# Turning the memory attention's outputs by transposing DMAs, as f16 halves, in a two-attention Trainium2 kernel

## The chip, the cores and the metric

One core of one Trainium2 chip runs the whole program. Its engines are TensorE (PE, with its weight loads shown as PEld), VectorE (DVE), ScalarE (ACT), GpSimd (POOL) and SyncE (SP), which here issues every DMA of the program. The metric is the device time of one execution in microseconds (us). The kernel before takes 1773.4 us, the median of three executions that lie between 1772.57 and 1774.67 us.

## The reference, cut to what matters

Two independent attentions over 2048 positions, 1024 features and 32 heads of 32; their outputs stand side by side. The change concerns A, which walks four segments of 512 positions with a compressive memory:

```python
for s in range(4):
    qs, ks, vs = q[:, :, s], k[:, :, s], v[:, :, s]
    p = softmax(qs @ ks.T * scale + mask)          # causal inside the segment
    a_dot = p @ vs
    pq = phi(qs)                                    # t+1 if t>0 else exp(t)
    a_mem = (pq @ M) / (pq @ z + 1e-6)              # M, z from the earlier segments
    outs.append(g * a_mem + (1 - g) * a_dot)
    M = M + phi(ks).T @ vs;  z = z + phi(ks).sum(0)
a = concat(outs) @ wo
```

B projects q, k and v, maps q and k through a per-head weight and two softmaxes (of +t and -t), forms linear attention with the sums over all positions, and projects with its own `wo`.

## The kernel before, in words

**Arithmetic.** Matrices are kept as two f16 tiles, a high half and the rest, and each product is made of three f16 matmuls (`product`, L352). To fit f16, a tensor is first scaled by a bound on its size (`halves`, L376: ScalarE writes the scaled high half, VectorE the scaled rest). B's projections and A's output projection use seven block products in place of eight (`strassen`, L541, and the last loop of the file).

**Stages.** First come A's 32 units, each one segment s (512 positions) of one group g of four heads (L582). Unit u is made by `produce` (L710: k, q and v projections, halves, three stacked copies of q and of k sent by DMAs at L727) and `attend` (L740). While unit u attends, the engines also produce unit u+1, fold B's feature weights (`fold`, L969) and load later weights. Then, for eight pairs of B's 128-row tiles, the k and v projections, softmaxes and sums (L1214 on); then, for 16 tiles, the q side and B's output projection (L1385 on). Here the normalised features are split into halves and turned by `dma_start_transpose` (L1440) before a matmul reads them. Last comes A's output projection: eight steps c of the loop at L1463, each with a row tile c and a row tile c+8.

**The place of the change.** At the end of `attend`, VectorE forms the local part in `osum` (L926), for s > 0 GpSimd adds the memory part `amem` (L930), and the sum, positions in partitions, must be turned so that features are in partitions. TensorE does this with four f32 transposes into a PSUM bank (L935), ScalarE copies the bank to `oT` (L603, through `copy`), and SP stores `oT` as f32 in the DRAM scratch `oa_d` (L937). The output stage loads two row tiles of `oa_d` (L1467), VectorE makes four sums and differences (L1473), and `halves` scales and splits seven operands by the reciprocal of one bound of the whole tensor, `osc2[:, 0]` (lines L386 and L388 in the profile); then come 7 x 12 matmuls at L1502. That bound is the running maximum `big` of the value bounds, filled in `bounds_v` (L673).

**What sets the order.** Nothing runs in the order in which it is written. Every `op(...)` gives an engine, an estimated duration, the buffers that it reads and writes, a priority `prio` (a lower number first), for DMAs a latency `lat` and a size `kb`. `Graph.run` (L148) simulates the engines with these numbers at build time: it takes the engine that can start earliest, and among what could start then the lowest `prio`. The result is a fixed order on each engine and on SP's queue; on the chip each engine follows its order and waits where something is late. A DMA's data is planned for its issue duration, plus a term for the bytes at 230 GB/s, plus `lat`. An `op` with `port=True` on VectorE and all on GpSimd are planned not to overlap. A tag with `bufs=1` has one buffer: the next user of the tag waits for all uses of the one before. The priority of unit u is 2u in `produce` and 2u+1 = P in `attend`.

```python
    def buf(self, pool, shape, dtype, tag, bufs=1):
        q = self.tags.setdefault(tag, [])
        b = Buf(lambda: self.pools[pool].tile(shape, dtype, name=tag, tag=tag, bufs=bufs),
                (q[-bufs] if len(q) >= bufs else None, q[-1] if q else None, self.opened.get(pool)))
...
                flow = max(flow, free[e]) + o.kb / self.FLOW
                o.lat += flow - free[e]
```

A's stage keeps its tiles in a pool "a" and B's in a pool "b" that takes the same memory; `G.control(swap, ["b"])` lets tiles of "b" be planned only once every operation listed before it has been started in the plan.

Of the kernel before, what the change touches and what calls it, by code (L numbers as in the profile page):

```python
# [8 lines left out]
F32 = mybir.dt.float32  # L9
# [234 lines left out]
def tile_kernel(ctx: ExitStack, tc: tile.TileContext, ax, aw, awv, awo, beta, bx, bwqk, bwv, bphi, bwo, out):  # L244
# [7 lines left out]
    oa_d = dram.tile([NT, 128, NG, 128], F32, name="oa_d")  # L252
# [46 lines left out]
    osc2 = const.tile([128, 2, 2], F32, name="osc2")  # L299
    nc.gpsimd.memset(causal[:, 0:384], 0.0)  # L300
# [295 lines left out]
    bigs, swfs, wscs, oscs, phss = (G.fixed(t) for t in (big, swf, wsc, osc2, phs))  # L596
# [76 lines left out]
    def bounds_v(k, segs, prio):  # L673
# [5 lines left out]
        for x in segs:  # L679
# [8 lines left out]
            big[:, 0:1], bv()[:, 1, a:a + 1], bv()[:, 1, b:b + 1], big[:, 0:1], op0=OP.max, op1=OP.max), r=w, w=[(bigs, 0)], prio=prio)  # L688
        op(POOL, 0.4, lambda: nc.gpsimd.tensor_scalar(bv()[:, 0, v], xsc[:, s0:s0 + n, 0], wvs[:, kk, 0:1], None, op0=OP.mult),
           r=[*((xscs, x) for x in segs), (wvss, kk)], w=w, prio=prio)  # L690

    def values(u):
# [7 lines left out]
        op(POOL, 0.39, lambda: nc.gpsimd.tensor_scalar(sc(), gate1[:, 4 * g:4 * g + 4], bv()[:, 1, i2:i2 + 1], None, op0=OP.mult),  # L700
           r=[gates, (bv, i2)], w=[sc], prio=P + VPRIO)
# [38 lines left out]
    def attend(u):  # L740
        s, g = units[u]
        d, P = un.pop(u), 2 * u + 1
        st, vl, vf, bd, bv, i2 = stk[u % 3], vlb[u % 2], vfb[u % 3], bds[group(u)], d["bv"], s % 2
        KR, QR = [(st, (1, r)) for r in range(3)], [(st, (0, r)) for r in range(3)]
# [71 lines left out]
        if s > 0:  # L816
            amem = G.buf("a", [128, 4, 4, 32], F32, "amem", 1)
            for b in range(2):
                ps = bank("misc", [128, 2, 132], "memory")
                for i in range(2):  # L820
# [5 lines left out]
                dve(0.1, lambda ps=ps, dm=dm: nc.vector.tensor_scalar(dm(), ps()[:, :, 128:132], 1e-6, None,  # L826
                                                                       op0=OP.add), r=[ps], w=[dm])
# [104 lines left out]
        oT = G.buf("a", [128, 4, 128], F32, "oT", 1)  # L932
        po = bank("misc", [128, 4, 128], "output")
        for i in range(4):
            pe(0.112, lambda i=i: nc.tensor.transpose(po()[:, i, :], osum()[:, i, :], ident), r=[osum], w=[po], need=[oT])  # L935
        act(0.48, copy(oT, po), r=[po], w=[oT])
        op(SP, 0.6, lambda: nc.sync.dma_start(oa_d[4 * s:4 * s + 4, :, g, :].rearrange("c p t -> p c t"), oT()),  # L937
           r=[oT], w=[(osc, u)], prio=P, lat=1.5)
# [446 lines left out]
    for c in range(NT):  # L1385
# [25 lines left out]
        for hb in range(2):  # L1411
# [27 lines left out]
            for a in range(2):  # L1439
                op(SP, 0.6, lambda a=a, eh=eh, hb=hb, pt=pt: nc.sync.dma_start_transpose(pt()[:, a], eh()[:, hb, a]),  # L1440
                   r=[(eh, (hb, a))], w=[(pt, a)], prio=P, lat=2.0, kb=256)
# [132 lines left out]
```

## Time and profile before

| | |
|---|---|
| median of three executions | 1773.4 us (1772.57 to 1774.67) |
| profiled execution, its own time | 1776.28 us |
| its span on the core | 1774.3 us |
| busy: PE, DVE, ACT, POOL | 1692.8, 1472.0, 1129.0, 942.9 us |
| mean granted TensorE clock | 0.987 |

The profiled execution took 2.9 us more than the median. "Busy" counts a matmul from its start to its modelled end, and consecutive matmuls overlap, so a PE that is busy all the time can still be short of its full rate. `L935` in a row is line 935 of the kernel; `misc<-ident,osum` names the tile written and the tiles read; `x128` is a count; after the bar of a group come busy time and the mean duration of one in ns, and after the next bar the engine's idle time just before them with what ended it. In a row of the stages, the numbers behind each engine are its busy time and, in brackets, its instructions. In a chain, the work that ended last is followed back through what released it.

### The profile page before, as it was taken

To read this page: it belongs to the slowest core of one execution; us is meant where nothing else is said; L and a number is where in the kernel's file an instruction comes from. 1 tells how busy PE (TensorE), PEld (TensorE's weight loads), DVE (VectorE), ACT (ScalarE), POOL (GpSimd) and SP (SyncE) were. 2 spreads that over 40 slices of the span, in tenths; PEclk is the share of its full clock that TensorE was granted. 3 is DMA by queue.
4 is the path that set the end of the run, shared out by engine and by line. 5 is a ranking of instruction groups with operands and counts; after the bars stand their busy time and mean duration, and the time that the engine had idled before them with its cause. 6 is when DMAs were issued, how large, how long until landed. Compare 5 with 4: busy or idle time off the path is not lost.

```text
span 1774.3 us, 38460 instructions
## 1 busy us (share of the span) xinstructions
PE 1692.8 (95%) x14456; PEld 1013.7 (57%) x14456; DVE 1472.0 (83%) x3335; ACT 1129.0 (64%) x2063; POOL 942.9 (53%) x1141
## 2 busy tenths in 40 slices
PE   7999998999999999999989998999889899999999
PEld 5767766677776766676644444444544344444444
DVE  6989989899787888788877999997999889887541
ACT  6897886988766878688673755554644454444431
POOL 6445454555757677867583544443467778640000
PEclk9999999999999999999989999999999999999999
DMA  6546545574545453665465344266455555565311
GB/s 204 175 144 182 161 144 161 167 222 141 148 139 150 112 158 107 173 210 144 153 192 203 113 160 161 90 234 243 153 139 132 158 146 148 137 190 172 119 66 65
DMA packets 240842, 275.67 MB, mean 155 GB/s; under 512 B 137488, under 2 KB 190480, under 8 KB 231952
## 3 DMA queue, kind: packets, MB, share of 16 engines
q1 hardware_dynamic: 240656, 273.22, 49.9%
q8 instruction: 113, 1.85, 0.4%
q14 instruction: 73, 0.60, 0.1%
HBM read 145.44 MB, written 85.00 MB: 130 GB/s over the span
## 4 chain that ended last, share of the span: by engine, by line
PE 46%; DVE 31%; ACT 5%; issue 3%; POOL 2%; DMA 2%; SPq 0%; DVEq 0%; ACTq 0%; POOLq 0%
PE proj L359 17%; PE proj L549 5%; PE proj L1502 5%; DVE r L1122 4%; DVE mx L1112 3%; DVE e L1116 3%; PE pv L903 3%; PE s L867 3%; PE s L1502 2%; DVE s L775 2%; DVE S L388 2%; PE s L769 2%; DVE e L1114 2%; DVE dn L1419 2%; DVE kls L1437 2%
## 5 line engine op out<-in xcount | busy, mean ns | idle before, releaser
L359 PE MATMUL proj<-S,S 128*128 128x128 f16 (+1 forms) x3072 | 503.1, 299 | 5.6 <-ACT S L386 3.6
L359 PEld LDWEIGHTS <-S 128*128 128x128 f16 x4608 | 331.4, 99 | 154.1 <-issue 9.7
L549 PE MATMUL proj<-S,S 128*128 128x512 f16 x1488 | 352.5, 385 | 24.3 <-ACT cs L555 12.1
L549 PEld LDWEIGHTS <-S 128*128 128x128 f16 x1968 | 189.5, 99 | 247.3 <-issue 35.2
L880 POOL TENSOR_SCALAR_AFFINE_SELECT ph<-ph 128x256 f16<-128x256 f16 (+1 forms) x448 | 197.1, 462 | 174.4 <-DVE ph L874 137.4
L874 DVE SCALAR_TENSOR_TENSOR ph<-s,ph 128x512 f16<-128x512 f32 x320 | 210.4, 683 | 58.3 <-ACT ph L873 56.4
L775 DVE CUSTOM_DVE_ANT_0 s<-s,causal 128x512 f32<-128x512 f32 (+3 forms) x512 | 242.2, 510 | 12.5 <-PE s L769 9.1
L871 ACT ACTIVATE s<-s,bd 128x512 f32<-128x512 f32 x320 | 212.2, 708 | 23.0 <-PE s L867 22.6
L873 ACT ACTIVATE ph<-s 128x512 f16<-128x512 f32 x320 | 189.9, 652 | 0.9 <-PE pv L903 0.3
L1119 ACT ACTIVATE e<-e,sk 128x256 f32<-128x256 f32 x256 | 114.6, 500 | 99.6 <-DVE e L1116 96.5
L359 PE MATMUL misc<-S,ot 128*128 128x512 f16 x768 | 172.4, 382 | 1.9 <-DVE ot L1454 1.4
L359 PEld LDWEIGHTS <-ot 128*128 128x128 f16 x768 | 74.0, 98 | 92.3 <-DVE ot L1454 2.4
L769 PE MATMUL s<-S 96*128 96x512 f16 (+3 forms) x512 | 113.3, 300 | 5.8 <-DVE mt L775 4.2
L867 PE MATMUL s<-S 104*128 104x512 f16 (+3 forms) x512 | 114.5, 302 | 1.2 <-DVE quad L1011 0.5
L1416 POOL TENSOR_TENSOR e<-e,zb 128x512 f32<-128x512 f32 x64 | 90.9, 1441 | 46.3 <-DVE r L1122 40.7
L359 PE MATMUL proj<-wv,S 128*128 128x128 f16 x1536 | 104.2, 221 | 0.3 <-DVE mt L775 0.3
L903 PEld LDWEIGHTS <-ph 128*128 128x128 f16 x2560 | 87.6, 96 | 17.9 <-issue 1.9
L1226 POOL TENSOR_TENSOR e<-e,r 128x1024 f32<-128x1024 f32 x32 | 64.5, 2020 | 61.2 <-DVE r L1125 50.4
L903 PE MATMUL pv<-vl,ph 128*128 128x66 f16 (+1 forms) x2560 | 92.7, 185 | 2.1 <-POOL ph L880 1.3
L1429 POOL TENSOR_TENSOR e<-e,r 128x1024 f32<-128x1024 f32 x32 | 67.4, 2113 | 37.7 <-DVE r L1427 34.4
L1122 DVE TENSOR_REDUCE r<-e 128x32 f32<-128x1024 f32 x64 | 76.8, 1204 | 9.8 <-ACT e L1119 9.8
L549 PE MATMUL s<-S,S 128*128 128x512 f16 x324 | 77.1, 379 | 1.8 <-ACT cs L555 1.8
(300 smaller groups left out, 3294.0 us busy)
## 6 DMA issues: line engine op xcount, KB each, us to landing
S<-h SPq DMA_DIRECT2D x192, 128.0 KB
S<-wf_d SPq DMA_DIRECT2D x21, 1024.0 KB
st<-bwqk SPq DMA_DIRECT2D x64, 256.0 KB
wf_d<-fo SPq DMA_DIRECT2D x48, 256.0 KB
out<-os SPq DMA_DIRECT2D x40, 256.0 KB
wf_d<-oT SPq DMA_DIRECT2D x36, 256.0 KB
S<-xf_d SPq DMA_DIRECT2D x9, 1024.0 KB
S<-aw SPq DMA_DIRECT2D x16, 512.0 KB
```

Of the source, the lines that this page charges most:

```text
L359: op(PE, dur, lambda c=c, a=a, b=b, lv=lv, rv=rv: nc.tensor.matmul(pv(), lv(), rv(), start=(c == 0 and a + b == 0), stop=(c == n - 1 and a ...
L549: op(PE, 0.215, lambda n=n, a=a, b=b, lv=lv, rv=rv: nc.tensor.matmul(ps(), lv(), rv(), start=(start and n == 0 and a + b == 0), stop=(n == ...
L769: nc.tensor.matmul(ps()[:, o:o + 128 * i + 128], st()[0:96, 0, h, 128 * i:128 * i + 128], st()[0:96, 1, h, 0:128 * i + 128], start=True, s ...
L775: dve(0.12 + 0.00113 * n, lambda h=h, i=i, o=o, n=n: nc.vector.tensor_tensor_reduce(ps()[:, o:o + n], ps()[:, o:o + n], causal[:, 512 - n: ...
L867: nc.tensor.matmul(ps()[:, o:o + n], st()[0:104, 1, h, 128 * j:128 * j + 128], st()[0:104, 0, h, 128 * j:512], start=True, stop=True)
L871: act(0.59, lambda: nc.scalar.activation(ps(), ps(), AF.Exp, bias=0.0, scale=bd()[:, 4, i2, 0:1]), r=[(bd, i2)], w=[ps])
L873: act(0.5, lambda: nc.scalar.activation(ph()[:, 0], ps(), AF.Copy, scale=2.0 ** 14), r=[ps], w=[(ph, 0)])
L874: dve(0.6, lambda: nc.vector.scalar_tensor_tensor(ph()[:, 1], ps(), 2.0 ** 14, ph()[:, 0], op0=OP.mult, op1=OP.subtract), r=[ps, (ph, 0)], ...
L880: nc.gpsimd.affine_select(pd, pd, pattern=[[0, n], [1, 128]], compare_op=OP.is_ge, fill=0.0, base=0, channel_multiplier=-1)
L903: nc.tensor.matmul(ps()[:, i, n0:n1], ph()[:, a, o:o + 128], vl()[:, j, h, n0:n1], start=(i == 0 and a == 0), stop=(j == min(i, 2)), skip_ ...
L1122: op(DVE, 1.13, lambda: nc.vector.tensor_reduce(r(), e(), axis=AX.X, op=OP.add), r=[e], w=[r], prio=prio)
L1502: op(PE, 0.215, lambda n=n, a=a, b=b: nc.tensor.matmul(ps(), v(a)[:, n, :], wform[w]()[:, b, n, :], start=(start and n == 0 and a + b == 0 ...
```

## The change

Per unit, the four TensorE transposes, their PSUM bank and ScalarE's copy out of it go. Instead ScalarE copies `osum` to an f16 high half, GpSimd subtracts to give the f16 rest, both in a tile `oh` on the tag "pkt" (the tag of the turned keys, one buffer), and SP issues one transposing DMA for each half into `oT`, now f16, and then the store to `oa_d`, which holds two f16 halves in the room of one f32. These operations have priority P + 3.2 in place of P.

The outputs are kept divided by a running maximum: `bounds_v` keeps in `top` the largest value bound up to each segment and in `part` the ratio of the segment's own bound to it; `sc` (the factor of the local part) uses `part`, and the memory part's denominator is multiplied by `top`. After B's q side, `top` is multiplied once by the reciprocal of the whole tensor's bound.

In the output stage each row tile is loaded as two quarter-size f16 pairs on the tag "cs"; VectorE adds each pair to f32, and ScalarE multiplies by `top` (two instructions for each pair). The sums and differences follow as before; the seven operands are then split without a scale (a ScalarE copy, a VectorE subtraction). All of this preparation has priority P - 1.5 in place of P. Lastly the planned duration of the existing transposing DMAs at L1440 is set from 0.6 to 1.25.

```diff
-    oa_d = dram.tile([NT, 128, NG, 128], F32, name="oa_d")
+    oa_d = dram.tile([NT, 2, 128, 4, 2, 128], F16, name="oa_d")
...
+        for x in segs:
+            op(DVE, 0.07, lambda x=x: nc.vector.tensor_tensor(
+                top[:, kk, x + 1:x + 2], top[:, kk, x:x + 1], bv()[:, 1, x % 2:x % 2 + 1], op=OP.max), r=w, w=[(tops, kk)], prio=prio)
+        op(DVE, 0.1, lambda: nc.vector.reciprocal(part[:, kk, s0:s0 + n], top[:, kk, s0 + 1:s0 + n + 1]), r=[(tops, kk)], w=[(parts, (kk, s0))], prio=prio)
+        op(DVE, 0.07, lambda: nc.vector.tensor_tensor(part[:, kk, s0:s0 + n], part[:, kk, s0:s0 + n], bv()[:, 1, v], op=OP.mult),
+           r=w, w=[(parts, (kk, s0))], prio=prio)
...
-        op(POOL, 0.39, lambda: nc.gpsimd.tensor_scalar(sc(), gate1[:, 4 * g:4 * g + 4], bv()[:, 1, i2:i2 + 1], None, op0=OP.mult),
-           r=[gates, (bv, i2)], w=[sc], prio=P + VPRIO)
+        op(POOL, 0.39, lambda: nc.gpsimd.tensor_scalar(sc(), gate1[:, 4 * g:4 * g + 4], part[:, k % 4, s:s + 1], None, op0=OP.mult),
+           r=[gates, *[(parts, (k % 4, y)) for y in ((0, 1) if s < 2 else (2,)) if y <= s]], w=[sc], prio=P + VPRIO)
...
-                dve(0.1, lambda ps=ps, dm=dm: nc.vector.tensor_scalar(dm(), ps()[:, :, 128:132], 1e-6, None,
-                                                                       op0=OP.add), r=[ps], w=[dm])
+                dve(0.1, lambda ps=ps, dm=dm: nc.vector.tensor_scalar(
+                    dm(), ps()[:, :, 128:132], 1e-6, top[:, kk, s + 1:s + 2], op0=OP.add, op1=OP.mult), r=[ps, (tops, kk)], w=[dm])
...
-        oT = G.buf("a", [128, 4, 128], F32, "oT", 1)
-        po = bank("misc", [128, 4, 128], "output")
-        for i in range(4):
-            pe(0.112, lambda i=i: nc.tensor.transpose(po()[:, i, :], osum()[:, i, :], ident), r=[osum], w=[po], need=[oT])
-        act(0.48, copy(oT, po), r=[po], w=[oT])
-        op(SP, 0.6, lambda: nc.sync.dma_start(oa_d[4 * s:4 * s + 4, :, g, :].rearrange("c p t -> p c t"), oT()),
-           r=[oT], w=[(osc, u)], prio=P, lat=1.5)
+        oh = G.buf("a", [128, 2, 512], F16, "pkt", 1)
+        oT = G.buf("a", [128, 4, 2, 128], F16, "oT", 1)
+        op(ACT, 0.52, lambda: nc.scalar.activation(oh()[:, 0], osum().rearrange("p c n -> p (c n)"), AF.Copy), r=[osum], w=[(oh, 0)], prio=P + 3.2)
+        op(POOL, 1.25, prio=P + 3.2, fn=lambda: nc.gpsimd.tensor_tensor(oh()[:, 1], osum().rearrange("p c n -> p (c n)"), oh()[:, 0], op=OP.subtract),
+             r=[osum, (oh, 0)], w=[(oh, 1)])
+        for a in range(2):
+            op(SP, 1.25, lambda a=a: nc.sync.dma_start_transpose(oT()[:, :, a, :], oh()[:, a]), r=[(oh, a)], w=[(oT, a)],
+               prio=P + 3.2, lat=2.0, kb=128)
+        op(SP, 0.6, lambda: nc.sync.dma_start(
+            oa_d[4 * s:4 * s + 4, g // 4, :, g % 4].rearrange("c p a t -> p c (a t)"), oT().rearrange("p c a t -> p c (a t)")),
+           r=[oT], w=[(osc, u)], prio=P + 3.2, lat=1.5)
...
+    op(DVE, 0.1, lambda: nc.vector.tensor_scalar(top, top, osc2[:, 0, 1:2], None, op0=OP.mult), r=[(oscs, 0)], w=[tops], prio=P)
...
-                op(SP, 0.6, lambda a=a, eh=eh, hb=hb, pt=pt: nc.sync.dma_start_transpose(pt()[:, a], eh()[:, hb, a]),
+                op(SP, 1.25, lambda a=a, eh=eh, hb=hb, pt=pt: nc.sync.dma_start_transpose(pt()[:, a], eh()[:, hb, a]),
...
-            op(SP, 0.6, lambda t=t, k=k: nc.sync.dma_start(t().rearrange("p h g t -> p (h g) t"), oa_d[k]),
-               r=[osc], w=[t], prio=P, lat=1.0, kb=512)
+            for h in range(2):
+                hl = G.buf("b", [128, 4, 2, 128], F16, "cs", 4)
+                op(SP, 0.6, lambda hl=hl, k=k, h=h: nc.sync.dma_start(
+                    hl().rearrange("p g a t -> p (g a t)"), oa_d[k, h].rearrange("p g a t -> p (g a t)")),
+                   r=[osc], w=[hl], prio=P - 1.5, lat=1.0, kb=256)
+                op(DVE, 0.6, lambda t=t, h=h, hl=hl: nc.vector.tensor_tensor(t()[:, h], hl()[:, :, 0], hl()[:, :, 1], op=OP.add),
+                   r=[hl], w=[(t, h)], prio=P - 1.5)
+                for i in range(2):
+                    op(ACT, 0.4, lambda t=t, h=h, i=i, k=k: nc.scalar.activation(
+                        t()[:, h, 2 * i:2 * i + 2], t()[:, h, 2 * i:2 * i + 2], AF.Copy, scale=top[:, 2 * h + i, k // 4 + 1:k // 4 + 2]),
+                       r=[*((tops, y) for y in range(4))], w=[(t, h)], prio=P - 1.5)
...
-               r=[A0, A1, *[(ss, i) for i in range(k)]], w=[(ss, k)], prio=P)
+               r=[A0, A1, *[(ss, i) for i in range(k)]], w=[(ss, k)], prio=P - 1.5)
...
-            halves(*hl, ((src, k) if src is ss else src, half(src, k)), (oscs, 0, lambda: osc2[:, 0]), 512, P)
+            op(ACT, 0.52, lambda hl=hl, src=src, k=k: nc.scalar.activation(hl[0][2](), half(src, k)(), AF.Copy),
+               r=[(src, k)], w=[hl[0][:2]], prio=P - 1.5)
+            op(DVE, 0.6, lambda hl=hl, src=src, k=k: nc.vector.tensor_tensor(hl[1][2](), half(src, k)(), hl[0][2](), op=OP.subtract),
+               r=[(src, k), hl[0][:2]], w=[hl[1][:2]], prio=P - 1.5, port=True)
```

6 lines of the change are left out of this document (5 added, 1 removed).

## The prediction

> **What bounds the kernel now.** I read the busy times by stage first: A's units with a full pipeline, A's end, B's k side, B's q side, the join of that with A's output projection, and the projection.
>
> ```profile
> 60.00:860.00 800.00, 787.62 (x8550) 561.07 (x8548) 685.01 (x1956) 630.82 (x1147) 488.63 (x758) 1.00 0.53 155
> 860.00:945.00 85.00, 76.91 (x658) 43.97 (x656) 67.39 (x162) 59.85 (x105) 55.97 (x81) 0.94 0.61 202
> 945.00:1300.00 355.00, 329.07 (x2167) 163.78 (x2166) 322.88 (x556) 196.30 (x406) 157.04 (x114) 0.99 0.46 166
> 1300.00:1600.00 300.00, 278.19 (x1845) 131.05 (x1844) 275.25 (x412) 139.13 (x250) 205.14 (x133) 0.99 0.55 149
> 1600.00:1625.00 25.00, 24.89 (x166) 11.69 (x166) 19.76 (x29) 12.50 (x19) 0.52 (x1) 0.93 0.68 211
> 1625.00:1774.00 149.00, 145.26 (x674) 65.68 (x671) 59.98 (x88) 50.30 (x77) 0.00 (x0) 1.00 0.23 85
> ```
>
> Behind each stretch and its length stand PE, PEld, DVE, ACT and POOL, then the granted clock, the DMA share and GB/s. From 60 to 860 PE idles 12.4 us in 800; DVE has 115 us left, ACT 169, POOL 311. From 945 to 1600 PE and DVE are both at 91 to 93%. From 1625 PE is full but for the last copy and store. So PE work taken out before 860 can shorten the program, work added to ACT, DVE or POOL there should find room, and the output stage gets shorter only if its matmuls do.
>
> Then PE's waits between 60 and 860, to see whether an engine that is about to get more work already holds PE up, and the part of the chain that ended last behind 1600.
>
> ```profile
> PE s L769 <- DVE mt L775: 4.2, 9, 0.9
> ...
> PE misc L837 <- POOL sc L700: 0.5, 1, 0.5
> ...
> PE misc L795 <- DVE mh L790: 0.2, 1, 0.2
> ```
>
> ```profile
> by line: PE proj L1502 47.6%; PE s L1502 23.8%; PE misc L359 13.1%; PE misc L1502 11.9%; DMA pt<-kls 2.9%; PE pv L1448 1.4%; ACT os L1509 0.4%; issue 0.1%; ACTq L1509 0.0%
> ```
>
> The columns of the waits are us in all, times and the longest. The table has 18 rows, from the first to the last shown; the row with POOL is the only one with it, all the others name DVE, and none names a DMA. The chain behind 1600 has no preparation of the output stage in it, only matmuls, one DMA of the q side and the last copy.
>
> **The change, part by part.**
>
> (1) The transposes. Four instances in a row, and what follows them on PE:
>
> ```profile
> 559.85 0.60 PE L935 MATMUL misc<-ident,osum 128*128 128x128 f32 x4
> 560.28 0.50 PE L822 MATMUL misc<-mem,pq 128*128 128x132 f32 x3
> ...
> 60.00:860.00 800.00, 17.56 (x116) 13.44 (x116) 1.00 0.53 155
> 860.00:945.00 85.00, 1.81 (x12) 1.42 (x12) 0.94 0.61 202
> ```
>
> The next matmul starts 0.43 us after the first transpose: that is what a unit's four transposes take from PE. Their busy time alone, in the last two rows, is 17.56 us for 116, 0.61 a unit, but its ends overlap the next matmul's start, so 0.43 is the price and 0.61 the upper end. 116/4 = 29 units lie before 860: 29 x 0.43 = 12.5 us (17.6 at most; 0 if something else paces the units). The three units behind 860 lie where PE has 8 us of idle; I count nothing for them.
>
> (2) Copies and subtractions in the units. Rows of the same forms:
>
> ```profile
> L603 ACT ACTIVATE oT<-misc x32: 577/597/777, 88.8 to 942.2; 128x512 f32<-128x512 f32 x32
> L1256 ACT ACTIVATE pt<-e x64: 613/622/632, 966.6 to 1272.4; 128x512 f16<-128x512 f32 x64
> L1259 POOL TENSOR_TENSOR pt<-e,pt x32: 1152/1162/2712, 968.8 to 1269.0; 128x512 f16<-128x512 f32 x32
> L683 DVE TENSOR_SCALAR bv<-misc x9: 150/152/160, 28.4 to 714.3; 128x2 f32<-128x2 f32 x7, 128x1 f32<-128x1 f32 x2
> L826 DVE TENSOR_SCALAR dm<-misc x48: 111/160/167, 91.3 to 915.7; 128x8 f32<-128x8 f32 x48
> ```
>
> ACT exchanges 0.597 for 0.622, 0.8 us in 32 units. POOL gains 32 x 1.162 = 37 us, against 311 idle. What stands behind a subtraction on POOL is mostly the causal masks (L880) that PE's `pv` waits for; if each subtraction delayed PE by its whole length it would cost 37 us, but POOL is 61% busy and none of PE's waits above is on a mask, so I take 0. `bounds_v` runs 9 times (the count of L683) and gains 16 maxima, 9 reciprocals and 9 products, 34 x 0.152 = 5.2 us of DVE, hidden in its 115 (5.2 if not). `dm` gets a second operation in an instruction of 0.16 us that stays one instruction: 0.
>
> (3) The DMAs. The trace has transposing DMAs of twice the size in the q side, and shows how long after its issue the matmul behind one starts:
>
> ```profile
> L1440 SPq DMA_TRANSPOSE pt<-kls x64: 1231/1248/5174, 1290.8 to 1607.6; - x64
> ...
> 1427.06 1.23 SPq L1440 DMA_TRANSPOSE pt<-kls  x1
> ...
> 1431.06 0.86 PE L1448 MATMUL pv<-pt,st 128*64 128x128 f16 x24
> ...
> 1595.09 1.23 SPq L1440 DMA_TRANSPOSE pt<-kls  x1
> ...
> 1600.11 0.61 PE L1448 MATMUL pv<-pt,st 128*64 128x128 f16 x15 [3.52 <-DMA pt<-kls]
> ```
>
> 64 new ones take 64 x 1.25 = 80 us of SP (40 if half the bytes halve the issue; I take 80, the row's own value), and the data is there 4.0 us after the start of the issue, or 5.0 behind a load: 2.8 to 3.8 us behind its end. Three things wait: the store behind them on SP, with every DMA behind it, above all the stacked copies of q and k (L727); the next unit's turned keys, on the tag "pkt"; and the fold's halves on the tag "oT". SP waits already, in the same stretch of the program:
>
> ```profile
> SPq L962 <- POOL oT L466: 56.8, 15, 10.9
> SPq L962 <- POOL ph L880: 52.8, 19, 8.5
> SPq L937 <- ACT oT L603: 48.9, 21, 9.1
> SPq L727 <- ACT h L721: 40.7, 16, 11.0
> ```
>
> These come to 199 us, with PE hardly waiting, so the plan keeps distance between SP and PE, and the store's own wait on ScalarE (48.9) goes for one on a DMA. A unit takes 800/29 = 27.6 us, and the keys need their tag once in it. I take 1 us for new stalls (0 to 40: one issue of 1.25 us on PE's path in each of 32 units; a gain is excluded, since SP gets only more).
>
> The Trainium skill speaks against this part: VectorE: DVE Perf Modes, section The three transpose paths, gives 390 ns for a 128x128 transpose on TensorE and 1309 ns by DMA, and its rules for kernel authors take TensorE where PSUM will do. The trace has 270 ns for one on TensorE, pitch 0.11, and 1.25 us of issue for eight blocks by DMA. An estimate by that page, eight half-blocks of a unit each 1309 ns on the path, is 10.5 us a unit, 335 us in all; Advanced Engine Details and Errata, section X-Bar Transpose, has them as fast as ordinary DMAs instead. What decides is not the transfer but who waits for it.
>
> (4) The hand-over to B. Tiles of "b" are planned only once the last store is.
>
> ```profile
> 939.39 1.27 POOL L930 TENSOR_TENSOR osum<-osum,amem 128x512 f32<-128x512 f32 x1 [2.49 <-DVE osum L926]
> ...
> 942.17 2.75 PE L549 MATMUL misc<-S,S 128*128 128x512 f16 x12
> 942.65 0.59 ACT L555 ACTIVATE cs<-proj 128x512 f32<-128x512 f32 x1
> 944.70 0.39 SPq L937 DMA_DIRECT2D oa_d<-oT  x1
> 944.76 2.75 PE L549 MATMUL s<-S,S 128*128 128x512 f16 x12
> 947.35 1.03 PE L549 MATMUL proj<-S,S 128*128 128x512 f16 x4
> ```
>
> `osum` is done at 940.66; then 0.62 (copy), 1.16 (subtraction), 1.25 (issue) and 2.8 (landing) put the store at 946.5, against 944.70, and the first copy into "b", now 942.65, up to 4 us later. PE has two products of 2.59 us (942.17, 944.76) that need no tile of "b" as cover; I take +2 (0 to 4).
>
> (5) The output stage.
>
> ```profile
> L1119 ACT ACTIVATE e<-e,sk x256: 492/498/516, 957.2 to 1582.5; 128x256 f32<-128x256 f32 x128
> L1473 DVE TENSOR_TENSOR zb<-e x8: 679/684/1923, 1599.1 to 1676.5; 128x512 f32<-128x512 f32 x8
> L386 ACT ACTIVATE ot<-e,osc x16: 706/712/723, 1582.9 to 1721.7; 128x512 f16<-128x512 f32 x16
> L388 DVE SCALAR_TENSOR_TENSOR ot<-e,osc,ot x16: 744/748/754, 1587.7 to 1722.5; 128x512 f16<-128x512 f32 x16
> ```
>
> A step gains 4 x 0.684 on DVE and loses 7 x (0.748 - 0.684): +2.3 us, 18 in eight steps, on a stretch where DVE is busy 60.0 of 149. ACT gains 8 x 0.498 and loses 7 x (0.712 - 0.622): +3.4, 27 in all, on 50.3. PE keeps its 84 matmuls a step, 145.26 us for eight, so the stage stays at PE's length. If that cover were gone the cost would be 27. The first step is prepared while the q side, at 92% of DVE, ends: its four additions (2.7) and eight copies (4.0) can stand ahead of the last tile's output copies. I take +1 (0 to 4).
>
> (6) The planned 1.25 at L1440 removes and adds nothing; it lets the plan order the q side otherwise. The nearest rows are the DVE's 24.8 us of idle in those 300 and the wait of 3.5 at 1600.11: -10 to +10, since no reason excludes either sign; I take 0.
>
> Sum: -12.5 + 1 + 2 + 1 = -8.5. The profiled execution of 1776.28 (span 1774.3 and 2.0 around it) would become 1767.8; it lies 2.9 over the median, so the median goes from 1773.4 to 1764.9, say 1765.
>
> **The rivals.**
>
> *The transposes paid on SP's queue (slower).* SP issues in order, and a store that waits 2.8 us or more for its transposes holds the stacked copies of the next q and k. The point from which it decides is 0.43 us of PE wait a unit. With one issue of 1.25 in each unit's path: -12.5 + 32 x 1.25 + 3 = +30, 1804; with half of it 1784. For it: up to 10.9 us of one wait on this queue, and the 5174 ns of one issue. Against it: the PE waits above, none on a DMA. The page that prefers TensorE would give this side. Chance 0.14.
>
> *PE does not pace the units (no change).* Busy time counts overlapping ends, and if the units hang on the exchange between scores and DVE, the 12.5 us turn into idle time: 1773.4 + 1 (in the terms above, +4 at most). For it: DVE's 86%, and the wait on `mt` as the longest. Against it: 12.4 us of idle in 800. Chance 0.15, at 1774.
>
> *The reordered B stages lose.* Stages of PE and DVE at 92% may lose by another order: 1765 + 10 + 2 = 1777. Chance 0.07; the same reorder as a gain, 1765 - 10 = 1755, has 0.12.
>
> **How the numbers follow.** My forecast itself has 0.52, with its own range of 1759 to 1769.8: from 0.61 a unit with nothing lost to two thirds of the gain. 0.2% of the time before, 3.5 us, is about what a measurement of this kernel can tell from no change. Faster: 0.52 + 0.12 = 0.64. Same: 0.15, less a little that falls over the line, and near misses of the forecast: 0.15. Slower: 0.14 + 0.07 = 0.21. The range from 1753 to 1784 holds the forecast, the gain, the unchanged case, the reorder and the smaller price of the queue; the full price, some 0.1, and a tail below stay out.
>
> **What would show it.** Right: no matmul at L935 and PE as full as before in the units, which reach B's k side some 10 us earlier; then equal lengths of B's stages, and a projection of 145 us on PE without gaps. Wrong: waits of PE on a DMA or on the keys' bank, longer waits of L727 on SP, `pv` waiting for masks behind a subtraction, a gap of PE where "b" opens, or a first output step that waits for its additions and copies.

## The result and the profile after

The changed kernel takes 1779.65 us (median of six executions, 1774.76 to 1781.28), the kernel before beside it 1774.51 (six, 1772.57 to 1775.26). The ratio is 1.0028 with a 95% interval of 1.0015 to 1.0041: slower by 0.3%, where 1765 was forecast. The time lies inside the stated range of 1753 to 1784, on the side that had a chance of 0.21. The profiled execution of the changed kernel took 1779.33 us, its span is 1777.4 (before 1774.3), its mean granted clock 0.983 (before 0.987).

The busy times by stage of the changed kernel, in the columns used before:

```profile
60.00:860.00 800.00, 779.15 (x8399) 545.58 (x8396) 696.37 (x1994) 631.05 (x1140) 508.01 (x781) 0.98 0.60 163
860.00:945.00 85.00, 77.88 (x674) 45.36 (x672) 69.43 (x170) 61.70 (x108) 65.08 (x89) 0.98 0.72 208
945.00:1300.00 355.00, 329.77 (x2156) 163.66 (x2155) 323.06 (x546) 195.41 (x406) 156.32 (x118) 0.98 0.49 170
1300.00:1600.00 300.00, 282.57 (x1874) 132.83 (x1873) 277.67 (x431) 146.69 (x263) 201.42 (x134) 1.00 0.61 156
1600.00:1625.00 25.00, 22.18 (x152) 10.26 (x152) 23.51 (x34) 16.26 (x33) 4.62 (x2) 0.93 0.52 133
1625.00:1777.00 152.00, 148.40 (x688) 67.07 (x686) 71.94 (x111) 63.34 (x119) 0.00 (x0) 1.00 0.26 90
```

The transposes are gone, yet the units are not shorter. From 60 to 945 PE executed 8399 + 674 = 9073 matmuls, before 9208; the difference of 135 is the 128 transposes and seven more, so by the records both kernels stand at about the same place at 945. PE idles 885 - 857.0 = 28.0 us in this stretch against 20.5 before, and the trace has it at half clock for 30.7 us there against 17.1. If PE does half as much in a stretch at half clock, the 13.6 us more cost 6.8, an estimate. So 7.5 of idle time and these 6.8, 14.3 together, stand against the 32 x 0.43 = 13.8 us of transposes. The saving is spent where it was made.

The rest moved little. VectorE's last local part starts at 943.0 (938.6 before), the first copy into "b" at 947.5 (942.65), the last matmul of the q side ends at 1616.4 (1612.2), and from there to the end are 161.0 us (162.1).

PE's waits from 60 to 945 now have 26 rows in place of 23; the first four, and the one on the keys' tile:

```profile
PE pv L914 <- POOL ph L891: 3.3, 5, 1.1
PE misc L806 <- DVE mh L801: 3.0, 4, 1.4
PE pv L914 <- DVE ph L885: 2.9, 6, 1.2
PE s L780 <- DVE mt L786: 2.8, 4, 1.8
...
PE misc L853 <- ACT pkt L606: 0.4, 1, 0.4
```

Masks on GpSimd (L891) now lead; before they made 1.3 us in three waits. Waits on a DMA, none before, come to 1.7 us in two, and the one on the keys' tile to 0.4, so little says that a DMA or the keys hold PE up. That is misleading, as the experiments show: PE's order is written at build time, so work that the plan had to put later isn't waited for on the chip; PE does other work first and runs out of it later. What shows it is progress, for instance how many of the 24 turned keys (the copies into `pkt`) were made by 430.5 us. First the kernel before, then the changed one, in the rows by tile:

```profile
L603 ACT ACTIVATE pkt<-misc x15: 578/643/842, 46.8 to 430.4; 128x512 f32<-128x512 f32 x15
```

```profile
L606 ACT ACTIVATE pkt<-misc x12: 575/598/777, 48.7 to 423.3; 128x512 f32<-128x512 f32 x12
```

Three keys fewer. The 430.5 is set just behind the fifteenth key of the kernel before; the changed kernel makes its fifteenth at 476.8. The first and second half of the units show what that does to PE, before and after:

```profile
60.00:430.00 370.00, 360.19 (x3879) 258.26 (x3877) 335.97 (x925) 305.29 (x555) 186.52 (x313) 0.99 0.55 166
430.00:860.00 430.00, 427.42 (x4672) 302.81 (x4671) 349.04 (x1032) 325.53 (x593) 302.11 (x445) 1.00 0.51 146
```

```profile
60.00:430.00 370.00, 350.75 (x3633) 241.19 (x3630) 334.57 (x944) 299.46 (x540) 185.25 (x320) 0.96 0.61 169
430.00:860.00 430.00, 428.40 (x4768) 304.39 (x4766) 361.79 (x1051) 331.60 (x600) 322.76 (x462) 1.00 0.59 157
```

From 430 on PE is full in both kernels. Before 430 its idle time grows from 9.8 to 19.3 us and its clock falls from 0.99 to 0.96.

The reason can be followed in the timelines (start, duration, engine, line, operation). First the second unit's keys and the first unit's outputs, before and after:

```profile
66.88 0.60 ACT L603 ACTIVATE pkt<-misc 128x512 f32<-128x512 f32 x1
...
88.78 0.60 ACT L603 ACTIVATE oT<-misc 128x512 f32<-128x512 f32 x1 [2.87 <-PE misc L935]
```

```profile
93.32 0.63 ACT L945 ACTIVATE pkt<-osum 128x512 f16<-128x512 f32 x1 [2.33 <-DVE osum L937]
...
103.96 0.60 ACT L606 ACTIVATE pkt<-misc 128x512 f32<-128x512 f32 x1
```

The buffer of a tag goes round in the order in which the program lists its users, and the first unit's halves are listed ahead of the second unit's keys. Before, keys ran ahead of the outputs of the unit before; now they stand behind them. In the changed kernel every copy of a unit's keys starts behind the halves of the unit before, and so it does in all its draws below.

Then a stretch of the changed kernel on ScalarE's `pkt` tiles and SP's queue:

```profile
254.71 0.72 ACT L606 ACTIVATE pkt<-misc 128x512 f32<-128x512 f32 x1
261.69 0.63 ACT L945 ACTIVATE pkt<-osum 128x512 f16<-128x512 f32 x1 [1.04 <-DVE osum L937]
...
268.99 0.55 SPq L977 DMA_DIRECT2D wf_d<-oT  x1
...
277.61 0.55 SPq L977 DMA_DIRECT2D wf_d<-oT  x1
...
285.22 2.54 SPq L949 DMA_TRANSPOSE oT<-pkt  x2
...
293.20 0.57 ACT L606 ACTIVATE pkt<-misc 128x512 f32<-128x512 f32 x1
```

The outputs take the one buffer of "pkt" at 261.69, right behind the keys of 254.71. Before they can be turned they need the one buffer of "oT", which fold's halves use for two more stores; the transposes go out at 285.22, and the next keys are copied at 293.20. Keys are 38.5 us apart here, where the pace of a unit is 27.6; these, the eighth, come at 293.20, and before at 229.1. In 11 of the 32 units the halves lie in "pkt" for over 10 us before the second transpose is issued, at most 35.5. The outputs hold "oT" longer too: from ScalarE's copy to the issue of the store the median unit takes 0.6 us before, and from the first transposing issue to that of the store 6.4 after.

The hand-over to B:

```profile
943.02 0.68 DVE L937 TENSOR_TENSOR osum<-oall,rd 128x512 f32<-128x512 f32 x1
943.78 1.27 POOL L941 TENSOR_TENSOR osum<-osum,amem 128x512 f32<-128x512 f32 x1 [2.49 <-DVE osum L937]
945.08 0.63 ACT L945 ACTIVATE pkt<-osum 128x512 f16<-128x512 f32 x1 [0.66 <-POOL osum L941]
945.79 1.16 POOL L946 TENSOR_TENSOR pkt<-osum,pkt 128x512 f16<-128x512 f32 x1 [0.74 <-ACT pkt L945]
946.72 2.93 SPq L949 DMA_TRANSPOSE oT<-pkt  x2
947.46 0.57 ACT L558 ACTIVATE cs<-proj 128x512 f32<-128x512 f32 x1
...
954.55 0.37 SPq L951 DMA_DIRECT2D oa_d<-oT  x1
```

The store goes out 9.9 us later than before (944.70), but the first copy into "b" follows the last local part by 4.4 us, 0.4 more than before (942.65 - 938.6): the new store doesn't hold it up.

The output stage: the added preparation by line (count, min/median/max ns, first and last start), and PE's waits at the join, 1590 to 1640.

```profile
L1488 DVE TENSOR_TENSOR e<-cs x32: 678/684/1229, 1581.7 to 1690.6; 128x512 f32<-128x512 f16 x32
L1491 ACT ACTIVATE e<-e,top x64: 492/496/510, 1583.0 to 1692.3; 128x256 f32<-128x256 f32 x64
```

```profile
PE pv L1464 <- DMA pt<-kls: 3.5, 2, 2.6
PE misc L362 <- DVE ot L1470: 1.2, 1, 1.2
PE proj L1530 <- ACT ot L1521: 0.9, 1, 0.9
PE proj L1530 <- DVE ot L1523: 0.3, 1, 0.3
PE misc L362 <- ACT ot L1468: 0.2, 1, 0.2
```

The durations are those of the forecast. At the join, 2.6 us of waits on late halves are new beside the 3.5 that were there (before, one wait of 3.5 on the same DMA); behind it PE is full.

### The profile page after: what moved, and what is told of

Same layout as the page of the kernel before. It is cut to its first block, busy times and chain, and to the rows that moved or that the text cites. A ratio compares the mean times of both kernels' runs of the same rounds, so it can differ in the third digit from the quotient of the medians.

```text
span 1777.4 us, 38464 instructions
## 1 busy us (share of the span) xinstructions
PE 1691.2 (95%) x14328; PEld 1001.3 (56%) x14328; DVE 1502.1 (85%) x3403; ACT 1153.1 (65%) x2127; POOL 970.2 (55%) x1173
## 5 line engine op out<-in xcount | busy, mean ns | idle before, releaser
L552 PE MATMUL proj<-S,S 128*128 128x512 f16 x1488 | 347.2, 382 | 12.6 <-ACT cs L558 7.9
L891 POOL TENSOR_SCALAR_AFFINE_SELECT ph<-ph 128x256 f16<-128x256 f16 (+1 forms) x448 | 192.0, 449 | 163.2 <-DVE ph L885 145.7
L786 DVE CUSTOM_DVE_ANT_0 s<-s,causal 128x512 f32<-128x512 f32 (+3 forms) x512 | 243.5, 507 | 20.3 <-PE s L780 16.8
L884 ACT ACTIVATE ph<-s 128x512 f16<-128x512 f32 x320 | 186.2, 637 | 0.7 <-PE pv L914 0.2
L552 PE MATMUL s<-S,S 128*128 128x512 f16 x324 | 78.9, 385 | 3.8 <-ACT cs L558 3.8
```

The source lines that it names most:

```text
L552: op(PE, 0.215, lambda n=n, a=a, b=b, lv=lv, rv=rv: nc.tensor.matmul(ps(), lv(), rv(), start=(start and n == 0 and a + b == 0), stop=(n == ...
L786: dve(0.12 + 0.00113 * n, lambda h=h, i=i, o=o, n=n: nc.vector.tensor_tensor_reduce(ps()[:, o:o + n], ps()[:, o:o + n], causal[:, 512 - n: ...
L884: act(0.5, lambda: nc.scalar.activation(ph()[:, 0], ps(), AF.Copy, scale=2.0 ** 14), r=[ps], w=[(ph, 0)])
L891: nc.gpsimd.affine_select(pd, pd, pattern=[[0, n], [1, 128]], compare_op=OP.is_ge, fill=0.0, base=0, channel_multiplier=-1)
```

## The experiments

All medians stand beside the kernel before on the same chip (1774.2 to 1775.8); ratios carry a 95% interval. Two questions are asked: what each part costs with the order of the instructions kept, and what the order does.

**The transposes alone, in the order before.** The four matmuls keep their places in the plan but aren't executed, and ScalarE copies `osum` itself.

```diff
-            pe(0.112, lambda i=i: nc.tensor.transpose(po()[:, i, :], osum()[:, i, :], ident), r=[osum], w=[po], need=[oT])
-        act(0.48, copy(oT, po), r=[po], w=[oT])
+            pe(0.112, lambda: None, r=[osum], w=[po], need=[oT])
+        act(0.48, copy(oT, osum), r=[po], w=[oT])
```

> The kernel before, in its own order, with the four transposes of each unit not executed: ScalarE copies osum itself, so A's outputs are stored unturned and A's result is meaningless; all else is kept. If PE paces the units (the prediction's part 1), 12.5 us go: 1762, at most 17.6. If chains of the other engines pace them in a fixed order, under 4 us go: 1771 to 1774.

1767.26 us, 0.9954 (0.9939 to 0.997): 7.5 us off by the medians, between the two cases expected. Then the same with the order planned anew, without the transposes and their bank:

```diff
-        po = bank("misc", [128, 4, 128], "output")
-        for i in range(4):
-            pe(0.112, lambda i=i: nc.tensor.transpose(po()[:, i, :], osum()[:, i, :], ident), r=[osum], w=[po], need=[oT])
-        act(0.48, copy(oT, po), r=[po], w=[oT])
+        act(0.48, copy(oT, osum), r=[osum], w=[oT])
```

> The same work left out (outputs unturned, A's result meaningless), but the order is planned anew without the transposes and their bank. If PE paces the units and a new order costs nothing, the same 1762 as with the old order. If a new order moves the time by itself, the two differ by 5 us or more, either way.

1764.63 us, 0.994 (0.9923 to 0.9957): 10.1 us off, 2.6 from the run with the old order. PE does pace the units, at least in part, and its transposes are worth 7.5 to 10 us by the medians, less than the 12.5 of the sum; the second interval reaches 13.7, and it is one order of many. So the change loses some 12 to 15 us elsewhere.

**The added work, in the order after.** GpSimd's subtraction becomes a memset of the low half:

```diff
-        op(POOL, 1.25, prio=P + 3.2, fn=lambda: nc.gpsimd.tensor_tensor(oh()[:, 1], osum().rearrange("p c n -> p (c n)"), oh()[:, 0], op=OP.subtract),
+        op(POOL, 1.25, prio=P + 3.2, fn=lambda: nc.gpsimd.memset(oh()[:, 1], 0.0),
```

> The changed kernel in its own order; GpSimd writes zeros for the low half in place of the subtraction, so the low halves of the memory attention's outputs are left out. If GpSimd's 32 subtractions of 1.16 us hold up DVE's small instructions and the masks, 5 to 10 us come back: 1770 to 1775. If the time is lost in the order and in the shared buffers, under 3 us: 1777 to 1780.

1774.94 us, 1.0003 (0.9993 to 1.0012), against 1.0028 for the change: 0.25%, some 4.4 us, come back when the instruction shrinks from 1.158 to 0.524 us. That lies between the two cases expected.

Plain DMAs in place of the transposing ones:

```diff
-            op(SP, 1.25, lambda a=a: nc.sync.dma_start_transpose(oT()[:, :, a, :], oh()[:, a]), r=[(oh, a)], w=[(oT, a)],
+            op(SP, 1.25, lambda a=a: nc.sync.dma_start(oT()[:, :, a, :], oh()[:, a].rearrange("p (c n) -> p c n", c=4)), r=[(oh, a)], w=[(oT, a)],
```

> The changed kernel in its own order; each transposing DMA is a plain DMA of the same bytes, so A's outputs are stored unturned and A's result is meaningless. If the transposing DMAs' 1.25 us of issue and their landing hold the SP queue on PE's path, 5 to 15 us come back: 1765 to 1775. If SP's waits are only idle time of the queue, under 3 us: 1777 to 1780.

1777.09 us, 1.0013 (1.0002 to 1.0023). The issues of the two kernels, the changed one first:

```profile
L949 SPq DMA_TRANSPOSE oT<-pkt x64: 1188/1244/2500, 94.0 to 948.4; - x64
```

```profile
L949 SPq DMA_DIRECT2D oT<-pkt x64: 599/629/1337, 94.2 to 948.8; - x64
```

SP's 64 issues take half the time, and 0.15% (2.7 us) comes back, with intervals that overlap: the case of under 3. So the length of the issues isn't where the time is. The order on the queue, and how long a DMA at its head waits for its data, are the same in both runs and aren't tested by this.

Both replacements together:

> The changed kernel in its own order with both left out: zeros for the low halves and plain DMAs in place of transposing ones (A's outputs stored unturned and without their low halves). If the two costs in the same order add up, 4.7 + 2.5 = 7 us come back: 1772 to 1773, and what is left to the 1767 of the kernel before without its transposes is the order's. If they are one and the same idle time, 5 us: 1775.

1776.24 us, 1.0012 (1.0002 to 1.0021): 0.16% back, 2.8 us, less than the memset alone gave and below both cases expected; the interval overlaps that of the change. The effects don't add up, and none of them reaches the missing 12.

The output stage without ScalarE's 64 scalings by `top`, whose places in the plan stay:

```diff
-                    op(ACT, 0.4, lambda t=t, h=h, i=i, k=k: nc.scalar.activation(
-                        t()[:, h, 2 * i:2 * i + 2], t()[:, h, 2 * i:2 * i + 2], AF.Copy, scale=top[:, 2 * h + i, k // 4 + 1:k // 4 + 2]),
+                    op(ACT, 0.4, lambda: None,
```

> The changed kernel in its own order without ScalarE's 64 scaling copies in the output stage, so A's outputs stay unscaled and A's result is wrong. If these copies hold up the last tiles of the q side (the step priced +1, at most 4), 2 to 4 us come back: 1775.5 to 1777.5. If they hide, under 1 us: 1779 to 1780.

1777.98 us, 1.0017 (1.0003 to 1.0031): 0.11% back, not told apart from none and between the two cases expected. What is missing isn't in the length of these instructions; the order is tried next.

**Other orders of both kernels.** Every planned duration is multiplied by a random factor between 0.99 and 1.01. The instructions stay the same; the plan comes out in another order.

```diff
+import random
+NOISE = random.Random(1)
...
-        o.eng, o.dur, o.fn, o.prio, o.lat, o.kb = eng, dur, fn, (prio, len(self.ops)), lat, kb
+        o.eng, o.dur, o.fn, o.prio, o.lat, o.kb = eng, dur * (1 + 0.01 * NOISE.uniform(-1, 1)), fn, (prio, len(self.ops)), lat, kb
```

> The kernel before, the same instructions; each planned duration is multiplied by a random factor between 0.99 and 1.01 (first draw), so that the builder arrives at another order. If a new order by itself moves the time by as much as the change did, this lies 3 us or more from 1774.5, either way. If the order hardly matters, within 2 us.

> As the first draw of the kernel before, with a second draw: 1770 to 1780 if orders scatter by some 5 us; within 2 us of 1774.5 if they hardly matter.

> The kernel before, third draw: 1769 to 1781 as its other orders.

The kernel before, seeds 1 to 3: 1780.67 us, 1.0029 (1.0017 to 1.0041); 1770.83, 0.9972 (0.9955 to 0.9989); 1762.73, 0.9932 (0.9913 to 0.9952). The third lies 6 us under the range expected for it.

> The changed kernel, the same instructions, its planned durations multiplied by the same kind of random factors (first draw). If the change as such costs what was measured, about 5 us over the kernel before with its draw. If the change binds orders by its shared single buffers and its own order is a fortunate one, 10 to 25 us over the kernel before's draws: 1785 to 1800. If the order is all, it lies among the kernel before's draws.

> As the first draw of the changed kernel, with a second draw: 1785 to 1800 if the shared buffers bind the orders; 1775 to 1785 if the change costs what was measured with any order.

> The changed kernel, third draw of random factors. If its own order is a fortunate one among those that its buffers allow, 1790 to 1810 as the other two draws. If the first two draws were bad luck, 1775 to 1785.

The changed kernel: 1810.31 us, 1.0191 (1.0155 to 1.0227); 1799.66, 1.0131 (1.0102 to 1.0161); 1806.51, 1.0179 (1.0159 to 1.0199). The first lies 10 us over the 1785 to 1800 expected.

Identical instructions spread over 18 us by their order, more than all that was forecast of the change. But the two kernels' draws don't overlap: 1771.4 on average before, 1805.5 after. By these averages of three the change costs some 34 us, and the changed kernel as it stands, 26 us below its draws, has a fortunate order. The own order of before lies inside its draws.

**Own buffers.** First only the halves leave the keys' tag, for a tag "os" whose buffer lies in another pool:

```diff
-        oh = G.buf("a", [128, 2, 512], F16, "pkt", 1)
+        oh = G.buf("stage", [128, 2, 512], F16, "os", 1)
```

> The changed kernel with the halves alone on a buffer of their own (the idle output tile of the stage pool), the turned halves still on the fold's tag; first draw. If sharing the keys' buffer is what binds, about as low as with both buffers (1761 to 1787); if sharing the fold's binds, 1800 to 1810 as the changed kernel's draws; if each does half, 1780 to 1795.

> The changed kernel with the halves alone on a buffer of their own, second draw. If each of the two shared buffers does about half, the three draws average 1785 to 1795; if the keys' buffer does nearly all, under 1782; if the fold's, over 1798.

> The same, third draw: the three draws average 1785 to 1795 if each shared buffer does about half, under 1782 if the keys' buffer does nearly all, over 1798 if the fold's.

1786.25 us, 1.0065 (1.0045 to 1.0085); 1799.32, 1.014 (1.0111 to 1.017); 1800.86, 1.0149 (1.012 to 1.0179): 1795.5 on average, half a microsecond over the range for "half each". Draw by draw that is 24.1, 0.3 and 5.7 us below the changed kernel, so on the time alone this step isn't told apart from the scatter of orders. Then `oT` has a tag of its own too; to make room, `ph` goes from six buffers to five:

```diff
-            ph = G.buf("a", [128, 2, 512], F16, "ph", 6)
+            ph = G.buf("a", [128, 2, 512], F16, "ph", 5)
...
-        oh = G.buf("a", [128, 2, 512], F16, "pkt", 1)
-        oT = G.buf("a", [128, 4, 2, 128], F16, "oT", 1)
+        oh = G.buf("stage", [128, 2, 512], F16, "os", 1)
+        oT = G.buf("a", [128, 4, 2, 128], F16, "oT2", 1)
```

> The changed kernel with buffers of their own for the new tiles (the halves on the idle output tile of the stage pool, the turned halves on a new tag; to make room the probability halves have five buffers in place of six), first draw of random factors. If the shared single buffers bind the orders, it lies 15 us or more under the changed kernel's draw (1810): below 1795, and three such draws lie around the kernel before's. If the new operations themselves cost the time, within 8 us of the changed kernel's draws.

> The same kernel with its own buffers, second draw: 15 us or more under the changed kernel's draws (1800 to 1810) if the shared buffers bind the orders, within 8 us of them if not.

> The same kernel with its own buffers, third draw: 15 us or more under the changed kernel's draws (1800 to 1810) if the shared buffers bind the orders, within 8 us of them if not.

1760.69 us, 0.9926 (0.9903 to 0.9949); 1787.26, 1.0071 (1.0043 to 1.0099); 1779.87, 1.0032 (1.002 to 1.0045): 1776.0 on average, 30 below the shared tags; draw by draw 49.6, 12.4 and 26.6, of which the second misses the 15 asked for. Even so the average lies 4.5 us above that of the kernel before and not below it. The first of them beats both kernels as they stand; the best order of before, at 0.9932, can't be told from it.

The traces of these orders say what the tags did. Each column gives the kernel's own order, where it was run, and the draws 1, 2, 3:

| | before | after | halves on "os" | both on own tags |
|---|---|---|---|---|
| time, us | 1774.5; 1780.7, 1770.8, 1762.7 | 1779.7; 1810.3, 1799.7, 1806.5 | 1786.3, 1799.3, 1800.9 | 1760.7, 1787.3, 1779.9 |
| keys made by 430.5 us | 15; 15, 15, 15 | 12; 12, 13, 12 | 15, 15, 15 | 15, 15, 15 |
| PE busy of 370, 60 to 430 | 360.2; 363.1, 365.4, 366.5 | 350.8; 352.3, 352.8, 348.5 | 360.8, 362.3, 355.8 | 365.9, 364.4, 362.5 |
| last keys copied, at us | 849; 842, 843, 837 | 895; 896, 903, 913 | 841, 838, 857 | 845, 824, 846 |
| last fold copy into "oT" | 904; 897, 898, 884 | 913; 912, 921, 931 | 908, 903, 921 | 846, 831, 866 |
| first copy into "b" | 942.7; 946.0, 938.4, 933.7 | 947.5; 955.9, 962.5, 971.4 | 952.0, 945.1, 963.6 | 917.9, 925.3, 941.1 |
| from there to the end | 831.7; 830.2, 831.4, 829.7 | 829.9; 850.0, 836.2, 833.7 | 835.0, 852.6, 836.6 | 839.9, 859.8, 835.7 |

The keys' tag: with the halves elsewhere the keys are back on their old times in all three draws (the second at 66 to 68 us, the fifteenth at 415 to 430, in place of 94 to 105 and 473 to 478), and PE gets most of its busy time before 430 back. The fold's tag: with `oT` elsewhere fold ends some 63 us earlier, and the gap that late folds leave in front of "b" narrows: PE is busy for 64.5, 67.7 and 69.2 of the 85 us from 860 with the halves on "os", for 78.9, 73.5 and 75.2 with both. The rows from 860 to 945 of draw 1, halves on "os" first, then both:

```profile
860.00:945.00 85.00, 64.50 (x479) 33.65 (x477) 50.96 (x121) 53.41 (x97) 56.04 (x78) 0.78 0.62 184
```

```profile
860.00:945.00 85.00, 78.91 (x533) 39.95 (x531) 63.75 (x135) 50.96 (x93) 46.84 (x61) 0.96 0.75 221
```

On average of three draws "b" opens at 939.4 before, 963.3 after, 953.6 with the halves on "os", 928.1 with both: 9.7 us for the keys' tag (3.9 to 17.4 by draw), 25.5 for the fold's (19.8 to 34.1). The 25.5 need not all be a price of the change. The kernel before already keeps its outputs and the fold's halves on the one buffer of "oT"; an `oT` of its own frees fold of the outputs altogether, so that it starts at 84 to 92 us and ends at 848 on average, where before it starts at 129 to 130 and ends at 893. With both free, B starts 11.3 us earlier than before. The kernel before without its transposes opens 9.1 us earlier (933.5), so the saving of the transposes may be what shows here, but the freed fold may be as well: the kernel before with an `oT` of its own wasn't run. What the one buffer less of `ph` does wasn't told apart either, and the changed kernel's own order wasn't run with own buffers.

Not settled: the last row of the table. Behind the opening, the changed kernel's draws need 9.6 us more than before's on average, and 11.0 and 14.7 more with own buffers, while its own order needs 1.8 less. The traces, split at the last matmul into `kv` and the last of the q side, say where: from the latter to the end all 14 take 161 to 165 us. Of the 9.6, 6.0 lie in the q side and 2.3 in the k side; of the 11.0 with the halves on "os", all in the q side; of the 14.7, 7.2 and 6.6. The planned 1.25 at L1440 and the output preparation, which the plan mixes into the q side, are candidates for the q side's part; neither was tried alone.

## Why the prediction was wrong

**(1) The transposes, -12.5.** Right in kind: PE paces the units, and "PE does not pace the units" falls. Too large in size: -7.5 with the order kept, -10.1 with a new one, inside the bounds given (0 to 17.6). Part of the saving turns into idle time: with the transposes taken out and the order kept, PE idles 26.2 us from 60 to 945, against 20.5.

**(3) The DMAs, +1. This is the step that failed.** Its row was right: 64 issues of 1.244 us, landing 3.1 us behind their issue. It named the three that wait, the store, the keys on "pkt" and the fold on "oT", and then covered the second with "the keys need their tag once in it", 27.6 us a unit. The cover counted the transfers, not who must stand behind whom and for how long the tag is held. On the shared tag a unit's keys have to wait until the outputs of the unit before are turned, where they ran ahead of them before; the fifteenth keys come 46 us later. The halves carry a priority behind the next unit's attention and the production of the one after it (P + 3.2), and they wait for "oT" as well, so each tag holds up the other: "pkt" for up to 35.5 us. That the low priority lengthens the hold is argued; no run changed it. Taking both tags away brings 30 us of the 34 back, over three orders each; in front of B it is 9.7 us for the keys' tag and 25.5 for the fold's, and part of the latter may be a gain of the fold that the kernel before could have as well. In the kernel's own order the 12 to 15 us between the transposes' gain and the result, less what the small terms below hold, fit this (12 keys in place of 15), but no run with own buffers shows it there. The upper end of 40 held, but for another reason than one issue in each unit's path. That the time stayed inside the stated range is owed to the own order: the three other orders, at 1799.7 to 1810.3, lie outside it.

The rival of SP's queue, in whose place this comes, was not it: with issues of half the length 2.7 us come back, and SP's waits between 60 and 945 haven't grown where it was feared.

```profile
SPq L737 <- ACT h L731: 37.4, 14, 7.3
...
SPq L949 <- ACT vf L717: 20.3, 1, 20.3
...
SPq L951 <- DMA oT<-pkt: 10.2, 6, 4.1
```

L737 (before L727, 40.7) waits no longer than it did (191.6 us in all its rows, before 225.4), and the stores wait 10.2 us for their transposes in all. The longest wait, 20.3 us for a half at the head of the queue, ends at 334 us; the stacked copies behind it had nothing to send before that either, since ScalarE wrote their half from 334.5. The next, 18.4 us, ends at 221, and their half was written from 221.5. The Trainium skill prefers TensorE for a 128x128 transpose where PSUM will do (VectorE: DVE Perf Modes, Rules for kernel authors). The changed kernel is slower, the side that this rule would take, but not by the length of the DMAs: the runs with transposing and with plain DMAs lie within 0.15% of each other.

**(2) The additions, 0.** ScalarE and VectorE as expected. GpSimd's subtraction may not be free: 4.4 us of its upper bound of 37 come back when it is shortened, though only 2.8 with plain DMAs beside it. The wait named for it, `pv` on the masks, did grow, from 1.3 to 3.3 us, but in the run with the memset it is still 3.2:

```profile
PE pv L914 <- POOL ph L891: 3.2, 7, 1.1
```

So the masks wait because of the order, not for the subtraction's length, and which wait carries the 4.4 us isn't shown. VectorE instructions that last until a GpSimd instruction ends (last section) are a candidate.

**(4) The hand-over, +2.** 0.4; the store is late, but it isn't what the first copy into "b" waits for.

**(5) The output stage, +1.** 161.0 against 162.1 us from the last matmul of the q side: PE covers it, as reckoned. At the join 2.6 us of new waits appear, the predicted place; taking the 64 scalings away gains 0.11%, not told apart from none. This holds for the kernel's own order; what its draws lose behind the opening of "b" stays open.

**(6) The reorder, 0 with -10 to +10.** Another order was looked for in the q side alone, with a chance of 0.19 for both signs together. It is a matter of the whole program: random changes of at most 1% in the plan's durations move the kernel before by -12 to +5 us with nothing else changed. That is as large as the effect that was forecast, and by the draws it hides most of the 34 us in the changed kernel as it stands. Whether the planned 1.25 itself gains or loses stays open.

Of the signs named for "wrong", the longer `pv` waits came, though not from where they were expected; waits of PE on a DMA came as 1.7 us, and those on the keys' bank as 0.4 us, although the keys came 46 us late. In this program, whose order is planned, the shared buffers are paid in the order and hardly in a wait.

## What to carry to other kernels

Before a new tile is put on a one-buffer tag of a critical chain, ask which user must now stand behind it that ran ahead before, and add up how long it holds the buffer, from its first write to the landing of its last read with everything that this waits for, and not how long its instructions take. A low priority can be expected to lengthen that hold, which wasn't tried. A run that gives the new tile a buffer of its own also frees the old users, so the kernel before needs the same run beside it. Where the order comes from a planner, a PE saving is priced by a run with the order kept, and a verdict on a change by several orders of each kernel, since one order alone can be off by more than the change is worth. Look for progress (how many of a repeated step are done by a given time), for waits may not show what the plan has already moved back.

## What the runs showed of the hardware

**A gap of under 2 us can be followed by half clock on PE, and a longer one need not be.** The changed kernel around 408 us, first in windows of 5 us (the clock is the first number behind the five engines), then on VectorE, GpSimd and PE:

```profile
405.00:410.00 5.00, 3.18 (x22) 1.91 (x21) 4.88 (x16) 1.27 (x2) 3.76 (x7) 0.87 0.90 273
410.00:415.00 5.00, 3.59 (x12) 1.22 (x11) 4.97 (x16) 2.84 (x5) 1.82 (x3) 0.50 0.39 106
415.00:420.00 5.00, 3.69 (x14) 2.26 (x14) 4.75 (x14) 2.72 (x6) 0.60 (x3) 0.61 0.69 172
```

```profile
406.06 1.06 DVE L668 SCALAR_TENSOR_TENSOR bd<-bd 128x2 f32<-128x2 f32 x1
407.11 1.22 DVE L690 SCALAR_TENSOR_TENSOR big<-bv,big 128x1 f32<-128x1 f32 x1
408.25 0.69 DVE L786 CUSTOM_DVE_ANT_0 s<-s,causal 128x512 f32<-128x512 f32 x1
```

```profile
405.94 1.15 POOL L469 TENSOR_TENSOR oT<-quad,oT 128x512 f16<-128x512 f32 x1
407.06 1.26 POOL L941 TENSOR_TENSOR osum<-osum,amem 128x512 f32<-128x512 f32 x1
```

```profile
406.85 0.38 PE L780 MATMUL s<-S 96*128 96x512 f16 x1
409.05 0.58 PE L780 MATMUL s<-S 96*128 96x384 f16 x2 [1.82 <-DVE mt L786]
```

PE waits 1.82 us for `mt`; its clock is granted at half from 408.7, 1.4 us into this gap, to 418.9. The gap's length alone doesn't decide it: in the same trace a gap of 1.85 us from 1133.7 and one of 2.22 from 1369.6 leave the clock at 1.00, and so does one of 3.4 from 1043.7 in the first draw with own buffers. Stretches at half clock are 3.4, 6.8 or 10.2 us long in the changed kernel's trace. They sum to 61.4 us there and to 44.4 before; over the orders tried the sum goes roughly with the time (37.5 us in the draw of 1762.7, 54.6 in that of 1760.7, 85.3 to 99.0 in the three of the changed kernel at 1799.7 to 1810.3). A short starvation can thus cost more than its own length, which may be one reason why small losses don't add up. The Trainium skill (TensorE: Matmul & The Clock Gate, Why this matters for your kernels) sets the limit at idle gaps of over some 3 us. These traces don't keep to it on either side: half clock behind 1.82 us with thin work around it, full clock behind 3.4. The same page's section A second HAM failure mode: psum-queue depth-cycling names frequent micro-idling of PE as another way to half clock; whether that is what happened at 408 no run shows.

**A small VectorE instruction can last until a GpSimd instruction ends.** The two rows at 406.06 and 407.11, on two numbers and one number per partition, take 1.06 and 1.22 us; the median of the first line is 0.152. Each ends within 0.03 us of the GpSimd instruction that was running beside it. So do all seven of the 27 instances of these two lines that take over 0.8 us (0.90 to 1.22); the other 20 take at most 0.37. No run tried the cause.

**A transposing DMA's issue doesn't follow its bytes.** 1.244 us for the new ones, 1.248 for those of twice the size at L1440, and 0.629 for a plain DMA into the same tile.
